# A fused attention and Fourier-mixing kernel: the row blocks of a second column half in another order, fewer stored pieces, sums of b beside other projections

## The chip, the cores and the metric

The kernel runs on one core of one Trainium2 chip. The metric is the device time of one execution in microseconds (us). The kernel before was executed three times; its median is 2955.21 us, from 2953.21 to 2961.31 us. A further execution was taken by the hardware profiler: it took 2959.83 us, with a span of 2958.1 us from its first to its last instruction, and every view of the profile shows that one.

## The reference

Two layers with inputs of their own stand side by side in the output.

```
qkv = x @ wqkv                          # x 2048 x 1024, wqkv 1024 x 3072, 32 heads of 32
p   = softmax(q @ k.T * 32 ** -0.5)
A   = concat_heads(p @ v) @ wo          # 2048 x 1024

a   = x @ dft_hid_re.T ;  b = x @ dft_hid_im.T     # another x, 2048 x 1024
B   = dft_seq_re @ a - dft_seq_im @ b              # 2048 x 1024
out = concatenate([A, B], -1)
```

All is float32. The DFT matrices are ordinary inputs: the kernel multiplies by them.

## The kernel before, in words

**Products in pieces of three.** A float32 operand is split into a high part and a low part of a shorter float type: `halves` (L491) makes the high part by a cast (VectorE or ScalarE, L497 and L499) and the low part by a subtraction (GpSimd or VectorE, L502). `group` (L401) then issues three matmuls for each pair of 128 x 128 by 128 x 512 tiles (high by high, low by high, high by low) into one PSUM bank, all of them at L412. The left operand of a group is a `piece` (L508): 128 x 512 floats, raw, high ("h") and low ("l"); the high and low tiles come from two rings of four buffers each (`HR`, `LR`, L419). The right operand is `moving` (L534) and lies in numbered slots (`slot`, `take_slot`).

**Fewer products.** The matrix products use a seven-product scheme for 2 x 2 blocks (the products are numbered 1 to 7 and taken in `ORDER` = 1, 2, 5, 6, 7, 3, 4). Products 5, 6, 7 and 3 need sums of blocks. A sum is made from loaded blocks by `fetch` (L439, addition at L477), and sums that are needed again are stored to DRAM and loaded back.

**The stages**, in the order of TensorE's work list `fills`:

1. `qkv` (L622): the projections to q, k and v in twelve steps. Steps 0 to 4 make what the first heads need; step 5 is product 1 for the other five column blocks, 6 is product 2, 7 is product 6, 8 is product 5, 9 is product 3; steps 10 and 11 (products 7 and 4) do v and then q and k, eight blocks with four groups each. From about 200 us on attention runs beside it.
2. `dense1` (L1486), the sequence DFT of B on the 2048 x 1024 input before the hidden one. It has 14 outer products `(r, pp)`: r = 0 (cosine matrix) with seven pp, then r = 1 (sine matrix) with seven. For r = 0 an outer product is done as a plain 4 x 2 block product (L1611 to L1658): two column halves n, in each four row blocks m, in each two pieces (k = 0, 1) with four chunks, so 24 matmuls a group and 192 an outer product. For r = 1 the seven-product scheme is applied a second time (L1659 to L1675), 14 groups of 12 matmuls.
3. `dense2` (the hidden DFT) and the attention's output projection `project`, `project_end`.

Attention's matmuls are three streams (scores "S" at L1786, transposed scores "T" at L1908, values "V" at L1927), interleaved with the list `fills`.

**Pieces stored and read again.** For r = 0, column half n = 0 makes its eight pieces (raw, cast, subtraction) and stores each, high and low part, to `ha_d` (`keep_a`, L1243); n = 1 reads all eight back (`again`, L1580, loads at L1594). The stored pieces with keys 1, 2 and 4 are read once more for r = 1; those with key 0 are not. Beside r = 0, `aside_c` (L1267) makes eight further pieces an outer product for r = 1 (products 5, 6, 3 and 7): it loads blocks into three small tiles "c" (L1289), adds (L1295), splits (L1296, L1297) and stores two halves to `ha_d` (L1298). One call of `aside_c` follows each group. `a_piece` (L1236) would make a piece for r = 1 that was not stored so far, and store it too.

**Sums of b beside the projections.** `aside` (L1306) makes sums of blocks of the sine matrix that r = 1 needs: two loads (L1333), one addition (L1335), one store to `tg_d` or `tb_d` (L1341), in a slot of its own out of three. `todo_a` lists 64 of them (16 for each of the outer products 5, 6, 7 and 4); 30 are done, one after each q and k group of steps 5, 6 and 7. The others are made by `load_r` (L1527) when r = 1 needs them; a sum that was made ahead is loaded there as one block.

**Who orders the work.** A planner (`Plan`, L62) simulates the five engines while the kernel is built, and what it starts in its time is the fixed program order of each engine. TensorE takes the heads of the streams or the next entry of `fills`. On the other engines, the operation with the smallest `rank` among those that are ready goes first; a rank is the number of groups built so far, plus an offset: `AHEAD` = 2 for `aside`, `LATER` = 6 for `aside_c`, negative for the attention's small loads. A DMA is planned to end at `dma + kb / KB_US + LANDING` (L145) with `KB_US` = 360 KB/us, and SP may issue only while the planned DMA time is less than `QUEUE` ahead (L217). On the chip each engine works through its order and waits on semaphores; every load and store but a few is issued by SP, in that order.

Of the kernel before, what the change touches and what calls it, by code (L numbers as in the profile page):

```python
# [61 lines left out]
class Plan:  # L62
# [6 lines left out]
    OVERLAP = {"ACT": 0.13, "DVE": 0.08, "POOL": 0.08}  # L69

    SLACK = {("SP", "POOL"): 2.0, ("SP", "DVE"): 2.0, ("SP", "PE"): 2.0, ("POOL", "DVE"): 0.7}
    KB_US = 360.0
    LANDING = 1.6
    QUEUE = 1.0

# [54 lines left out]
    def start(self, o, e=None):  # L130
# [11 lines left out]
        if o.kb:  # L142
            for _ in range(o.lanes):
                t = max(self.free[e], self.lane[0])
                self.dma = max(self.dma, t) + o.kb / o.lanes / self.KB_US  # L145
                o.end = self.dma + self.LANDING
# [74 lines left out]
def kernel(  # L221
# [46 lines left out]
    def f(ap):  # L268
        return ap.bitcast(F32)
# [82 lines left out]
    TWO = {(1,q) for q in ORDER}  # L352
# [74 lines left out]
    def seq():  # L427
        return float(len(frees))
# [153 lines left out]
    def chunk(p, c):  # L582
        return p, lambda t: t[:, c, :]
# [22 lines left out]
    def accs(i):  # L606
        old, users = take_slot(i)
        box = {}

        def get():  # L610
            if "t" not in box:
                box["t"] = slot(i, [P, 2, NB], F32)
            return box["t"]

        return [Acc(get, old, users, k) for k in range(2)]
# [6 lines left out]
    def qkv():  # L622
# [46 lines left out]
        def acc(i):  # L669
            box = {}  # L670

            def get():
                if "t" not in box:
                    box["t"] = vp.tile([P, 2, NB], F32, name=f"acc{i}")
                return box["t"]

            return [Acc(get, [], [], k) for k in range(2)]
# [161 lines left out]
        def qk_group(x, W, b, n, order=None):  # L839
            p = STEPS[x][0]  # L840
            early = x < 5
            h = FIRST.get(p)
            if p == 1 and n == 0:
                if early:
                    X[2 * b], X[2 * b + 1] = acc(b)
                else:
                    X[2 * b], X[2 * b + 1] = accs(15 + b - PAIRS)

            group(((chunk(W[c], b) if x == 0 else chunk(W, c), (XS[x, 4 * n + c], whole)) for c in range(4)), 4,
                  gather(p, 2 * b + n, qk_result(b + 8 * h[0], 2 * h[1] + n, early) if h else None, early, None if b % 2 else SCALE), order)  # L850
            if 5 <= x < 8:
                aside((12, 13, 14))
            elif x == 10 and b < 0:
                aside((0, 1, 2))

        def v_group(x, t):
# [379 lines left out]
    def a_piece(pp, p, i):  # L1236
        s = lambda x: (si_d[0][pp][x - 5][i], si.setdefault((pp, x, i), []))
        terms = a_terms(pp, p, i)
        a = piece(terms, s(p) if p in (5, 6) else None)
        keep_a(a, pp, p, i)  # L1240
        return a

    def keep_a(a, pp, p, i):  # L1243
        rank = seq()
        kept_a[pp, p, i] = [op("SP", ISSUE, lambda k=k, t=t: nc.sync.dma_start(ha_d[pp][p][i][:, k * NB : k * NB + NB], f(t()).rearrange("p t c -> p (t c)")), [made], [u], rank, 256)
                            for k, (t, made, u) in enumerate(zip((a.hi, a.lo), a.made, a.users.lists))]
# [15 lines left out]
    def put_b(r, pp, j):  # L1262
        return pp, "b", r, j
# [37 lines left out]
    kept_a = {}  # L1301

    todo_a = [put_b(1, pp, j) for pp in ORDER if pp in (5, 6, 7, 4) for j in range(16)]
    AHEAD, EACH, LATER = 2, 1, 6

    def aside(places):  # L1306

# [178 lines left out]
    def dense1():  # L1486
        spare[0] = True

        outers = [(r, pp) for r in range(2) for pp in ORDER]
        xo, yo = ([[[] for _ in range(8)] for _ in range(2)] for _ in range(2))  # L1490
        R, M, L, XY = [], {}, {}, {}
        PURE = [r for r in range(2) if not any((r, q) in TWO for q in ORDER)]
        NR = 12
# [105 lines left out]
        for o, (r, pp) in enumerate(outers):  # L1599
            hh = QUAD.get(pp)  # L1600

            def place_of(h, i):
                pos = 4 * h[0] + 2 * i + h[1] if h else 0
                to = wrote = None
                if h and hh:
                    c, nt = 2 * h[0] + i, 2 * hh[1] + h[1]
                    to = g_d[r][hh[0]][nt][:, :, c, :].rearrange("t p c -> p t c")
                    wrote = g_st[r][hh[0]][nt]
                return (xo_d[r][pos], xo[r][pos]), (yo_d[r][pos], yo[r][pos]), to, wrote

            if (r, pp) not in TWO:  # L1611
                for n in range(2):
                    for m in range(4):
                        r1, i = divmod(m, 2)

                        def terms():
                            for k in range(2):
                                key = {(0, 0): 1, (0, 1): 2, (1, 1): 4, (1, 0): 0}[r1, k]
                                if (pp, key, i) in kept_a:
                                    a = again(pp, key, i)  # L1620
                                else:
                                    a = piece([a_outer(pp, m, k)])
                                    keep_a(a, pp, key, i)
                                if m == k == 0 and L.get((o, n, 7)) is None:
                                    for c in range(NR - 8, 8):
                                        load_l(2 * o + n, c)
                                for c in range(4):
                                    yield chunk(a, c), (L[o, n, 4 * k + c], whole)

                        pos = 4 * r1 + 2 * i + n  # L1630
                        if r in PURE and pp in (1, 5) and n == 0 and i == 0 and r1 == 0:
                            XY[pp] = [None] * 8
                        if r in PURE and pp in (1, 5) and XY[pp][pos] is None:
                            XY[pp][pos & 6 : (pos & 6) + 2] = accs((16 if pp == 1 else 12) + pos // 2)
                        group(terms(), 8, gather1(pp, *place_of((r1, n), i), XY[1][pos] if r in PURE else None, XY[5][pos] if r in PURE and pp in (5, 7, 4) else None))
                        g = 2 * o + n
                        for c in range(NR - 8):
                            if c * 4 // (NR - 8) == m:
                                load_l(g + 1, c)
                                if g == 27:  # L1640
                                    load_ab(0, c)
                        if m == 3:
                            if n and o < 13 and outers[o + 1] in TWO:
                                while todo_c and todo_c[0][1] != 5:
                                    aside_c()
                                todo_c.clear()
                            if n and o < 13 and outers[o + 1] in TWO:
                                begin(o + 1, range(8))
                        if m == 1 and n and r in PURE and pp == 4 and o < 13 and outers[o + 1] in TWO:
                            load_r(o + 1, 0, 0)  # L1650
                            load_r(o + 1, 0, 1)
                            for kk in range(4):
                                load_b(o + 1, 0, kk)
                            early.append(1)
                        if r == 0 and (1, pp) in TWO:
                            todo_c.extend((pp, p, i) for p in {(0, 2): (5, 6, 3, 7), (0, 3): (5, 6, 3, 7)}.get((n, m), ()))
                        aside_c()
                continue  # L1658
            for x, p in enumerate(ORDER):  # L1659
                if p == 1:  # L1660
                    X = accs(10)
                if p == 5:
                    Y = accs(11)
                for i in range(2):
                    a = again(pp, p, i) if (pp, p, i) in kept_a else a_piece(pp, p, i)
                    group(((chunk(a, c), (M[o, x, c], whole)) for c in range(4)), 4, gather2(pp, p, X[i], Y[i] if p not in (1, 2) else None, *place_of(QUAD.get(p), i)))
                    if x < 6:
                        for kk in (2 * i, 2 * i + 1):
                            load_b(o, x + 1, kk)
                    elif o == 13:  # L1670
                        begin(14, range(4 * i, 4 * i + 4))
                    elif outers[o + 1] in TWO:
                        begin(o + 1, (2 * i, 2 * i + 1))
                    elif i:
                        begin(o + 1, range(8))  # L1675
# [294 lines left out]
    for h in range(H):  # L1970
        if h + 1 < H:
            scores(h + 1)
        else:
            sums(h)
        result(h, *transposed(h))
    dense1()
    dense2()
    project_end()
# [8 lines left out]
    while nf < len(fills) or any(place[n] < len(s) for n, s in streams.items()):  # L1987
# [43 lines left out]
        if nf < len(fills):  # L2031
            o, first, left = fills[nf]
# [14 lines left out]
        if ok:  # L2047
            n = min(ok)[1]
            o = heads[n][0]
# [49 lines left out]
```

## Time and profile before

| what | us |
|---|---|
| median of three executions | 2955.21 |
| profiled execution, its own time | 2959.83 |
| span of the profiled execution | 2958.1 |
| TensorE busy | 2924.5 |
| VectorE busy | 2378.0 |
| ScalarE busy | 2370.3 |
| GpSimd busy | 1124.1 |

The DMA engines moved 758.78 MB, 257 GB/s over the span. In a view of stretches of time, each row gives a stretch, then for each engine its busy time and in brackets its instructions, then the clock granted to TensorE, the mean busy share of the 16 DMA engines and their GB/s. A row of waits gives who waited for whom, the sum, the times and the longest. PE is TensorE, DVE VectorE, ACT ScalarE, POOL GpSimd, SP the engine that issues DMAs ("SPq" its queue). Matmuls overlap in the records, so a stretch can look busy while fewer matmuls start in it: the counts in brackets are the better measure.

### The profile page before, as it was taken

Reading aid. Unit: us, or ns where it says so; the run is one execution under the profiler, and the core shown is the slowest. Engines: PE = TensorE matmul, PEld = TensorE weight load, DVE = VectorE, ACT = ScalarE, POOL = GpSimd, SP = SyncE. Lnnn points to the kernel's source line nnn. Section 1 sums busy time; section 2 is a strip of 40 time slices with the busy share of each in tenths; the row PEclk is TensorE's granted clock in tenths of the full one; section 3 lists DMA queues with packets and bytes.
Section 4 is the critical chain, followed back from the end, with each engine's and each line's share of the span. In section 5 each row is a group of like instructions: output and inputs, shape, how many; then the busy total and the mean of one; then the engine's idle time right before and its main releaser. Section 6 shows DMA issues by size and latency. Waiting matters only on the chain.

```text
span 2958.1 us, 47210 instructions
## 1 busy us (share of the span) xinstructions
PE 2924.5 (99%) x14776; PEld 2120.4 (72%) x14776; DVE 2378.0 (80%) x3249; ACT 2370.3 (80%) x4487; POOL 1124.1 (38%) x883
## 2 busy tenths in 40 slices
PE   9999999999999999999999999999999999999999
PEld 8887677677776776666777776767777777777677
DVE  7678788778877888887799888888778887888655
ACT  5358798888888898888888898889888988888631
POOL 2325344132233444333356666667223512333000
PEclk9999999999999999999999999999999999999999
DMA  9979968667879999999988778886556555775468
GB/s 367 351 236 321 331 220 267 222 216 237 283 249 304 331 344 331 333 323 327 299 264 257 246 257 258 260 275 192 148 164 195 168 187 174 249 236 170 152 225 290
DMA packets 510614, 758.78 MB, mean 257 GB/s; under 512 B 123134, under 2 KB 156158, under 8 KB 510238
## 3 DMA queue, kind: packets, MB, share of 16 engines
q1 hardware_dynamic: 510220, 755.61, 77.9%
q8 instruction: 120, 1.97, 0.3%
q14 instruction: 130, 1.06, 0.1%
q10 hardware_dynamic: 144, 0.13, 0.0%
HBM read 509.64 MB, written 245.91 MB: 255 GB/s over the span
## 4 chain that ended last, share of the span: by engine, by line
PE 85%; DMA 9%; DVE 3%; ACT 1%; SPq 1%; issue 1%; POOL 1%; DVEq 0%; POOLq 0%; ACTq 0%
PE pd L412 39%; PE psT L1908 14%; PE psS L1786 13%; PE pd L1927 13%; PE psT L412 5%; DMA ha_d<-c 2%; DVE negm L1792 1%; DMA g<-in_ct 1%; DMA raw<-in_ct 1%; ACT psS L1795 1%; DMA slot<-tg_d 0%; DMA h<-ha_d 0%; DMA tg_d<-slot 0%; DMA l<-ha_d 0%; DMA qs<-m_d 0%
## 5 line engine op out<-in xcount | busy, mean ns | idle before, releaser
L1792 DVE TENSOR_REDUCE negm<-psS 128x1 f32<-128x1024 f32 x1024 | 1241.9, 1220 | 194.8 <-PE psS L1786 188.7
L1912 ACT ACTIVATE pt<-psT 128x512 f32<-128x512 f32 x2048 | 1186.7, 664 | 254.7 <-PE psT L1908 252.3
L1795 ACT ACTIVATE psS<-psS,negm 128x1024 f32<-128x1024 f32 x1024 | 1182.4, 1155 | 73.8 <-DVE negm L1792 70.6
L412 PE MATMUL pd<-slot,h 128*128 128x512 f32 x3392 | 1155.4, 391 | 3.7 <-DVE e L682 3.0
L1908 PE MATMUL psT<-qs,ks 128*128 128x512 f32 x2048 | 806.2, 397 | 8.1 <-DMA qs<-m_d 4.3
L412 PEld LDWEIGHTS pd<-slot,h 128*128 128x128 f32 x3392 | 639.5, 189 | 138.4 <-DVE e L682 3.3
L412 PE MATMUL pd<-slot,l 128*128 128x512 f32 x1696 | 662.8, 391 | 5.1 <-DMA l<-ha_d 2.7
L1908 PEld LDWEIGHTS psT<-qs,ks 128*128 128x128 f32 x2048 | 383.1, 188 | 170.0 <-issue 54.5
L1786 PE MATMUL psS<-ks,qs 128*128 128x512 f32 x1552 | 476.0, 393 | 7.5 <-ACT psS L1795 7.4
L1927 PE MATMUL pd<-pt,vt 128*32 128x512 f32 x4096 | 460.4, 596 | 0.6 <-DVE e L977 0.2
L412 PEld LDWEIGHTS pd<-slot,l 128*128 128x128 f32 x1696 | 319.5, 188 | 73.3 <-DMA l<-ha_d 3.5
L502 POOL TENSOR_TENSOR slot<-raw,slot 128x512 fp32r<-128x512 f32 x151 | 193.7, 1290 | 434.5 <-DVE slot L499 100.3
L1786 PEld LDWEIGHTS psS<-ks,qs 128*128 128x128 f32 x1552 | 289.8, 188 | 74.5 <-ACT psS L1795 16.4
L1927 PEld LDWEIGHTS pd<-pt,vt 128*32 128x32 f32 x4096 | 123.6, 110 | 284.6 <-issue 265.4
L477 POOL TENSOR_TENSOR raw<-raw,g 128x512 f32<-128x512 f32 x143 | 184.9, 1296 | 358.7 <-DVE negm L1792 49.8
L1795 ACT ACTIVATION_READ_ACCUMULATOR psS<-psS,negm 128x1 f32 x1024 | 279.7, 273 | 0.0
L502 POOL TENSOR_TENSOR l<-raw,h 128x512 fp32r<-128x512 f32 x110 | 141.9, 1290 | 293.0 <-PE psT L1908 69.2
L502 POOL TENSOR_TENSOR slot<-slot,slot 128x512 fp32r<-128x512 f32 x149 | 190.2, 1292 | 139.6 <-DVE slot L502 29.6
L412 PE MATMUL pd<-slot,slot 128*128 128x512 f32 x780 | 212.0, 390 | 0.2 <-DVE e L734 0.2
L412 PEld LDWEIGHTS pd<-slot,slot 128*128 128x128 f32 x780 | 146.5, 188 | 31.1 <-DVE e L734 0.9
L1786 PE MATMUL psS<-ks,qx 128*128 128x512 f32 x496 | 151.6, 396 | 3.2 <-ACT psS L1795 1.8
L477 DVE TENSOR_TENSOR raw<-raw,g 128x512 f32<-128x512 f32 x133 | 100.9, 763 | 27.0 <-issue 7.1
(139 smaller groups left out, 2278.2 us busy)
## 6 DMA issues: line engine op xcount, KB each, us to landing
h<-ha_d SPq DMA_DIRECT2D x154, 256.0 KB
l<-ha_d SPq DMA_DIRECT2D x154, 256.0 KB
slot<-in_ct SPq DMA_DIRECT2D x112, 256.0 KB
ha_d<-c SPq DMA_DIRECT2D x112, 256.0 KB
qk_d<-e SPq DMA_DIRECT2D x52, 512.0 KB
qs<-qk_d SPq DMA_DIRECT2D x128, 192.0 KB
ks<-qk_d SPq DMA_DIRECT2D x128, 192.0 KB
raw<-in_ct SPq DMA_DIRECT2D x96, 256.0 KB
```

The costliest lines, as they stand in the source:

```text
L412: nc.tensor.matmul(box["ps"], a[1]((a[0].hi, a[0].lo)[u]()), b[1]((b[0].hi, b[0].lo)[v]()), start=k == 0, stop=k == n - 1)
L477: (nc.gpsimd if e == "POOL" else nc.vector).tensor_tensor(out=dest(), in0=dest() if a is None else a.get(), in1=other["q"] if "q" in other ...
L502: (nc.gpsimd if e == "POOL" else nc.vector).tensor_tensor(out=lo(), in0=raw(), in1=f(hi()), op=ALU.subtract)
L1786: nc.tensor.matmul(p[:, i * NB : i * NB + NB], (QX[0] if own else QS[h % 2])[:, qt * P : qt * P + P], KS[h % 2][:, c * 1024 + i * NB : c * ...
L1792: nc.vector.tensor_reduce(out=ST["negm"][:, c, qt : qt + 1], in_=box["p"], axis=AX.X, op=ALU.max, negate=True)
L1795: nc.scalar.activation(box["p"], box["p"], AF.Exp, bias=ST["negm"][:, c, qt : qt + 1], accum_out=ST["sums"][:, c, qt : qt + 1])
L1908: nc.tensor.matmul(box["p"], KS[h % 2][:, t * P : t * P + P], QS[h % 2][:, j * NB : j * NB + NB], start=True, stop=True)
L1912: nc.scalar.activation(box["t"], box["p"], AF.Exp)
L1927: nc.tensor.matmul(po["p"][j * DH : j * DH + DH, :], VT[h][:, k, :], box["t"], start=(k == t0), stop=(k == t), tile_position=(0, j * DH),)
```

## The change

For r = 0 the second column half takes its row blocks in the order 2, 3, 0, 1. The pieces of blocks 2 and 3, made last in the first half, are used again from their ring buffers (`stay`); only those of blocks 0 and 1 are read back. Pieces with key 0 are no longer stored. What hung on the row block's number (loads of the next right operands, the flush at the end) hangs on the turn instead. `a_piece` no longer stores. The sums of b follow only the first of each block's two q and k groups, in steps 5 to 8 (20 of them), and then every q and k group of step 10 (16, in slots 0 to 2): 36 in all. Two planner constants change: `KB_US` from 360 to 335, `LATER` from 6 to 3.

```
-    KB_US = 360.0
+    KB_US = 335.0
...
-            if 5 <= x < 8:
+            if 5 <= x < 9 and n == 0:
                 aside((12, 13, 14))
-            elif x == 10 and b < 0:
+            elif x == 10:
                 aside((0, 1, 2))
...
         a = piece(terms, s(p) if p in (5, 6) else None)
-        keep_a(a, pp, p, i)
         return a
...
-    AHEAD, EACH, LATER = 2, 1, 6
+    AHEAD, EACH, LATER = 2, 1, 3
...
             if (r, pp) not in TWO:
+                stay = {}
                 for n in range(2):
-                    for m in range(4):
+                    for turn, m in enumerate((2, 3, 0, 1) if n else (0, 1, 2, 3)):
                         r1, i = divmod(m, 2)
...
                                 key = {(0, 0): 1, (0, 1): 2, (1, 1): 4, (1, 0): 0}[r1, k]
-                                if (pp, key, i) in kept_a:
+                                if (m, k) in stay:
+                                    a = stay[m, k]
+                                elif (pp, key, i) in kept_a:
                                     a = again(pp, key, i)
                                 else:
                                     a = piece([a_outer(pp, m, k)])
-                                    keep_a(a, pp, key, i)
-                                if m == k == 0 and L.get((o, n, 7)) is None:
+                                    if key:
+                                        keep_a(a, pp, key, i)
+                                    if r1:
+                                        stay[m, k] = a
+                                if turn == k == 0 and L.get((o, n, 7)) is None:
                                     for c in range(NR - 8, 8):
                                         load_l(2 * o + n, c)
...
                         for c in range(NR - 8):
-                            if c * 4 // (NR - 8) == m:
+                            if c * 4 // (NR - 8) == turn:
                                 load_l(g + 1, c)
...
-                        if m == 3:
+                        if turn == 3:
...
-                        if m == 1 and n and r in PURE and pp == 4 and o < 13 and outers[o + 1] in TWO:
+                        if turn == 1 and n and r in PURE and pp == 4 and o < 13 and outers[o + 1] in TWO:
```

## The prediction, on record before the result

> **What bounds the kernel now.** First the page: how busy TensorE is, and the DMA line over 40 slices.
>
> ```profile
> span 2958.1 us, 47210 instructions
> PE 2924.5 (99%) x14776; PEld 2120.4 (72%) x14776; DVE 2378.0 (80%) x3249; ACT 2370.3 (80%) x4487; POOL 1124.1 (38%) x883
> DMA  9979968667879999999988778886556555775468
> ```
>
> TensorE looks full, and the change takes no matmul away, so a gain can only come from matmuls that start late. Overlapping records hide those; I count them. The chain of work gives the price of one instruction in an undisturbed run, 5.44 / 24 = 0.2267 us, and 4.43 / 40 = 0.1107 us for the V products:
>
> ```profile
> 24.88 5.44 PE psT L412 x24
> 282.45 4.43 PE pd L1927 x40
> ```
>
> Then the view of stretches, once for all instructions and once for the V products (L1927) alone. The counts in the first bracket are what to read.
>
> ```profile
> core 0: us, PE busy (x) PEld busy (x) DVE busy (x) ACT busy (x) POOL busy (x), PEclk, DMA share, GB/s
> 200.00:400.00 200.00, 192.26 (x922) 140.33 (x921) 157.21 (x200) 159.92 (x300) 91.53 (x71) 0.98 0.89 295
> 580.00:780.00 200.00, 200.00 (x1029) 145.28 (x1026) 165.53 (x226) 174.21 (x335) 51.41 (x41) 1.00 0.72 236
> 900.00:1300.00 400.00, 390.56 (x1986) 273.41 (x1979) 331.37 (x436) 347.98 (x658) 160.29 (x125) 1.00 0.98 330
> 1300.00:1500.00 200.00, 195.09 (x991) 136.72 (x990) 161.84 (x224) 169.27 (x325) 73.97 (x58) 0.99 0.94 307
> 1500.00:1800.00 300.00, 300.00 (x1553) 216.58 (x1555) 265.48 (x373) 265.98 (x513) 189.39 (x150) 1.00 0.80 258
> 1800.00:2000.00 200.00, 195.50 (x1014) 136.40 (x1007) 171.82 (x233) 169.99 (x324) 131.74 (x104) 0.98 0.83 266
> ```
>
> ```profile
> 200.00:400.00 200.00, 23.35 (x208) 0.98 0.89 295
> 580.00:780.00 200.00, 33.60 (x300) 1.00 0.72 236
> 900.00:1300.00 400.00, 68.07 (x608) 1.00 0.98 330
> 1300.00:1500.00 200.00, 34.07 (x304) 0.99 0.94 307
> 1500.00:1800.00 300.00, 52.37 (x468) 1.00 0.80 258
> 1800.00:2000.00 200.00, 39.34 (x344) 0.98 0.83 266
> ```
>
> Work done from 1500 to 1800: (1553 - 468) x 0.2267 + 468 x 0.1107 = 297.8 us, so 2.2 us are lost, 0.75 in 100: the normal state. The same sum gives 20.3 lost from 900 to 1300 (17.3 above normal), 10.6 from 1300 to 1500 (9.1 above), 15.1 from 200 to 400 (13.6 above), 10.0 from 1800 to 2000 (8.5 above), 1.5 from 580 to 780 (none). Some 48 us above normal in all; that is all there is to win.
>
> From 900 to 1500 r = 0 of the sequence DFT runs. What TensorE waits for from 750 to 1500 is spread out:
>
> ```profile
> PE psS L1786 <- ACT psS L1795: 5.1, 7, 1.2
> PE psT L1908 <- DMA qs<-m_d: 4.3, 3, 2.2
> PE psT L1908 <- ACT pt L1912: 3.7, 4, 1.2
> PE pd L412 <- DMA l<-ha_d: 0.6, 1, 0.6
> ```
>
> None of these says "the piece was late". But ScalarE and VectorE work in order, and their casts and sums of loaded blocks stand ahead of the exponentials; SP, in order too, issues the 16 KB load qs<-m_d between 256 KB ones. I read all of it as DMA time, because the queue has none left:
>
> ```profile
> 1000.00:1225.00 225.00, 219.40 (x1127) 152.21 (x1129) 190.22 (x252) 198.96 (x377) 97.13 (x76) 1.00 1.00 348
> ```
>
> Share 1.00 at 348 GB/s: that is the ceiling of this mix of loads and stores.
>
> **Does traffic explain the loss?** Counting transfers of 256 KB (0.262 MB) in the code for one outer product of r = 0: right operands 16 (product 1, 2, 3), 32 (7, 4) or 48 (5, 6); pieces 8, or 24 where they are sums; 16 stores and 16 loads of pieces in ha_d; 28 of `aside_c`; 8 stores of results except in 1, 5, 6; 11 for attention (a head moves 2,496 KB by the code, and 468 V products at 128 a head are 1.17 heads in 96 us). Products 5 and 6 come to 143, 7 to 135, 3 and 4 to 119, 2 to 103, 1 to 95. TensorE's pace for `fills` is
>
> ```profile
> 1500.00:1800.00 300.00, 174.95 (x601) 1.00 0.80 258
> ```
>
> 2.0 a us, so 192 matmuls last 96 us. At 348 GB/s products 5 and 6 need 143 x 0.262 / 0.348 = 107.7 us each, 12 too many, and 7 needs 101.7, 6 too many: 30 us, where these three stand (about 965 to 1270) and 17.3 us are lost. The others fit (119: 89.6 us).
>
> **Pieces that stay.** Four of eight pieces an outer product are not read back, and the two with key 0 are not stored: 8 loads and 4 stores. That is 12 of 143, and 56 loads and 28 stores in all:
>
> ```profile
> h<-ha_d SPq DMA_DIRECT2D x154, 256.0 KB
> l<-ha_d SPq DMA_DIRECT2D x154, 256.0 KB
> ha_d<-c SPq DMA_DIRECT2D x112, 256.0 KB
> ha_d<-h SPq DMA_DIRECT2D x56, 256.0 KB
> ha_d<-l SPq DMA_DIRECT2D x56, 256.0 KB
> ```
>
> I expect 126, 126, 112, 42 and 42 after. 5 and 6 then need 131 x 0.262 / 0.348 = 98.7 us, 3 too many; 7 needs 92.7 and fits. 30 becomes 6. Scaled to the measured 17.3 that leaves 3.5: **-14 us**. From 1300 to 1500 (307 GB/s, share 0.94) traffic fits on average; the stalls are local, and taking a tenth away may leave all 9.1 or none; I take half, **-4.5 us**. No other engine loses work: a piece read back had no cast and no subtraction. The buffers are no tighter: the four `h` and `l` buffers hold the pieces of blocks 2 and 3 until the second turn of the second half ends; the pieces of blocks 0 and 1 replace them one by one, loaded a group ahead as before. At the change of halves there are now no piece loads beside the four right operands that wait for the slots of the last group. The groups' sums go into accumulators of their own, so the order doesn't matter to them.
>
> **a_piece without a store** is worth nothing: ha_d<-c x112 is 7 x 8 pieces x 2, so each piece of r = 1 is already kept, and a_piece isn't reached.
>
> **Sums of b.** Each is two loads, an addition (20 of the 30 on GpSimd) and a store; the first fence is the view of tg_d and of L1335, the second TensorE's waits from 185 to 450.
>
> ```profile
> L1341 SPq DMA_DIRECT2D tg_d<-slot x30: 319/376/1604, 222.5 to 369.1; - x30
> L1335 POOL TENSOR_TENSOR slot<-slot x20: 1277/1288/1470, 220.7 to 366.3; 128x512 f32<-128x512 f32 x20
> ```
>
> ```profile
> PE pd L412 <- DVE e L682: 3.0, 1, 3.0
> PE pd L412 <- POOL l L502: 2.5, 1, 2.5
> ```
>
> Fifteen leave steps 5 to 7 (five return in step 8, to about 420 us): 45 x 0.262 = 11.8 MB of the 59 MB from 200 to 400 (295 GB/s x 200 us), a fifth. The two waits are for an evacuation and a low part, not for a sum; I take a fifth of 13.6, **-2.7 us**, between none and all. Sixteen come to the q and k groups of step 10 (580 to 780): 48 transfers, 12.6 MB, lift 236 to 299 GB/s. The nearest rows at such a rate, 295 and 307 GB/s, lose 13.6 and 9.1 us above normal in 200 us; the row at 258 loses none. So the price lies between 0 and 13.6; I take **+4**, well below the nearest rows, since a pair of pieces there feeds 48 matmuls where steps 5 to 9 need a new one after every 24. GpSimd has room (51 of 200 us). On SP the sums go ahead of loads for later groups; behind them wait the first right operands of r = 0, whose slots 0 to 2 they hold. The three slots take five or six sums each and should be free before 780. If not, three loads and splits (some 7 us) come on top. r = 1 saves the additions of six sums, beside a TensorE that loses nothing at 1500 to 1800: 0.
>
> **The two constants.** 360 KB/us is 368.6 GB/s, above the measured 348; 335 is 343.0, just below. The order planned with 343 should put fewer early waits into the in-order engines; I count this in the -4.5. At the start the queue moves more,
>
> ```profile
> 25.00:100.00 75.00, 75.00 (x333) 62.13 (x332) 55.85 (x78) 30.67 (x51) 23.26 (x18) 1.00 1.03 379
> ```
>
> but TensorE's order is a fixed list there and it is never idle: 0. A new plan also moves every chance stall, 1800 to 2000 among them: bounds +-8.5 (that stretch's excess), value 0. `LATER` 3 is the rival below.
>
> **Sum:** -14 - 4.5 - 2.7 + 4 = -17.2 from 2959.83, 2942.6. The profiled execution stands 4.6 above the median, so the forecast is 2955.2 - 17.2 = **2938 us**, its own range 2925 to 2947.
>
> **The clock.** Two of the three waits for qs<-m_d (the chain has these loads) stand just ahead of two stretches with a lower clock:
>
> ```profile
> 1226.53 4.38 DMA qs<-m_d
> 1398.73 3.33 DMA qs<-m_d
> ```
>
> ```profile
> 1225.00:1250.00 25.00, 23.23 (x115) 16.69 (x108) 19.80 (x30) 19.23 (x36) 5.58 (x5) 0.93 0.97 295
> 1400.00:1425.00 25.00, 22.89 (x96) 18.55 (x100) 16.34 (x18) 20.59 (x41) 7.57 (x6) 0.93 0.93 303
> ```
>
> 0.93 over 25 us is 1.75 us lost after a gap of about 2 us, so such a gap costs nearly double, and the losses above hold both halves. The Trainium skill, TensorE: Matmul & The Clock Gate, section "HAM oscillation — how this bites in real kernels", asks for "no PE-idle gaps >~3.4µs"; by it these two gaps (at most 2.2 us) would cost no clock, and the forecast without the 3.5 us would be 2941. The trace disagrees with that bound.
>
> **Rivals.** *Traffic isn't the limit of r = 0*: the waits at TensorE name ScalarE and a 16 KB load, and 10.6 us are lost from 1300 to 1500 where the queue isn't full. Then products 5 to 7 recover a third of the 14 us, 1300 to 1500 nothing, the new sums cost 4: -5 + 4 - 1 = -2, **2953**. Against it: the loss begins where the share reaches 1.00. The Trainium skill, DMA: Bandwidth & Descriptors, section "Bandwidth", measures 425 GB/s on a single core for large loads, and names some 358 GB/s as the HBM limit of a core; by 425, products 5 and 6 would need 88 us, nothing would be late, and this rival would hold. The trace, 348 at share 1.00, speaks for the second figure. Chance 0.18.
>
> *Slower: SP stuck on aside_c.* From 900 to 1500:
>
> ```profile
> SPq L1289 <- DMA ha_d<-c: 53.9, 32, 4.1
> ```
>
> SP stops until a store has landed before it may load the tile "c" again, 32 times of 48, and all that is behind it in its order waits: heads, right operands, qs<-m_d. With `LATER` 3 these loads stand three groups earlier in SP's order, nearer to their store. If every one of 48 waited 2.3 us instead of 1.1 (the longest is 4.1), the sum is 110 us. If the 26.4 us above normal all came from the 53.9 us (0.49 each), that is +27 on top of the sum, -17.2 + 27 = +9.8: **2965**. It decides from about 107 us of this wait (53.9 + (17.2 + 8.9) / 0.49). Against it: 343 GB/s also plans the landing later. Chance 0.15.
>
> *All stalls fall*: with the new rate also 1800 to 2000 (8.5) and most of 200 to 400, and no cost of the sums: -35, **2920**. Chance 0.14. The forecast keeps 0.53. That the change doesn't do what it says is excluded for the stores and loads, which the code counts, and true of a_piece.
>
> **Chances.** This kernel's executions differ by 0.3%, 8.9 us; less can't be told from no change. Faster: 0.51 of the forecast, 0.14, 0.02 of the first rival: 0.67. Same: 0.02 + 0.16 = 0.18. Slower: 0.15. Range 2918 to 2962: from the full recovery to short of the slow rival.
>
> **What would show it.** Right: 126, 126, 42, 42 transfers; 36 sums; from 900 to 1300 less than 8 us lost by the count and a DMA share under 0.95; 580 to 780 near 0.9 with under 7 us lost. Wrong: share still 1.00 from 1000 to 1225; the SP wait at L1289 above 90 us; clock rows under 1.00 at new places; a stall at the first groups of r = 0 near 780.

## The result, and the profile after

The changed kernel took 2926.59 us (median of 4 executions, 2922.56 to 2927.65) against 2955.90 (4 executions): ratio 0.9896, 95% interval 0.9879 to 0.9913, 29 us faster. The forecast was 2938, with a range from 2918 to 2962. The page of the profiled execution (2926.61 us):

```profile
span 2924.8 us, 47119 instructions
PE 2910.0 (99%) x14776; PEld 2116.9 (72%) x14776; DVE 2364.0 (81%) x3226; ACT 2363.7 (81%) x4489; POOL 1152.8 (39%) x904
DMA  9979958798768999999887677885456555775468
```

The span is 33.3 us shorter than that of the profiled execution before, which lay some 4 us above its median; TensorE's instructions are as many as before. So the count of instructions in each stretch has to show where the time went. The view of stretches, all instructions, then the V products alone (line 1932 of the changed kernel):

```profile
200.00:400.00 200.00, 199.83 (x976) 149.22 (x975) 167.50 (x217) 170.49 (x322) 82.46 (x64) 1.00 0.77 258
580.00:780.00 200.00, 199.87 (x1045) 142.29 (x1044) 167.28 (x229) 172.31 (x331) 75.68 (x59) 1.00 0.90 306
900.00:1300.00 400.00, 398.48 (x2063) 284.41 (x2062) 345.63 (x463) 358.52 (x684) 172.10 (x135) 1.00 0.93 311
1300.00:1500.00 200.00, 199.09 (x1035) 138.67 (x1035) 167.37 (x222) 177.04 (x340) 85.54 (x67) 1.00 0.87 284
1500.00:1800.00 300.00, 299.43 (x1551) 215.47 (x1550) 264.03 (x372) 263.86 (x508) 180.18 (x142) 1.00 0.77 247
1800.00:2000.00 200.00, 195.51 (x995) 138.24 (x994) 170.37 (x221) 173.98 (x333) 140.01 (x110) 0.99 0.77 245
```

```profile
200.00:400.00 200.00, 23.35 (x208) 1.00 0.77 258
580.00:780.00 200.00, 37.71 (x336) 1.00 0.90 306
900.00:1300.00 400.00, 71.77 (x640) 1.00 0.93 311
1300.00:1500.00 200.00, 37.71 (x336) 1.00 0.87 284
1500.00:1800.00 300.00, 52.92 (x472) 1.00 0.77 247
1800.00:2000.00 200.00, 34.91 (x296) 0.99 0.77 245
```

With the prediction's prices (0.2267 us, and 0.1107 for a V product) and its normal loss of 0.75 in 100, the loss above normal is now 1.4 us from 200 to 400 (13.6 before), 0.6 from 580 to 780 (0), 3.6 from 900 to 1300 (17.3), 2.8 from 1300 to 1500 (9.1), 7.3 from 1800 to 2000 (8.5). The first and the two of r = 0 make up -32.2 of the -33.3 us.

The waits of TensorE from 750 to 1500 had summed to some 14 us and now sum to some 2 us; from 1000 to 1225 the share of the DMA engines fell from 1.00 to 0.95 (second fence; the third is SP's wait from 900 to 1500):

```profile
PE psS L1791 <- ACT psS L1800: 0.8, 1, 0.8
PE psT L1913 <- ACT pt L1917: 0.7, 1, 0.7
PE pd L412 <- DVE l L502: 0.4, 1, 0.4
PE psT L1913 <- DMA qs<-m_d: 0.3, 1, 0.3
```

```profile
1000.00:1225.00 225.00, 223.48 (x1149) 160.00 (x1148) 196.54 (x267) 204.00 (x391) 102.65 (x80) 1.00 0.95 322
```

```profile
SPq L1288 <- DMA ha_d<-c: 55.5, 32, 3.0
```

The transfers are those forecast, 126 and 126 loads, 42 stores each of high and low parts, 36 sums:

```profile
h<-ha_d SPq DMA_DIRECT2D x126, 256.0 KB
l<-ha_d SPq DMA_DIRECT2D x126, 256.0 KB
```

```profile
L1244 SPq DMA_DIRECT2D ha_d<-h x42: 319/382/937, 738.1 to 1385.7; - x42
L1244 SPq DMA_DIRECT2D ha_d<-l x42: 319/382/1299, 738.6 to 1386.2; - x42
```

```profile
L1340 SPq DMA_DIRECT2D tg_d<-slot x32: 319/402/793, 222.6 to 651.1; - x32
```

```profile
L1340 SPq DMA_DIRECT2D tb_d<-slot x4: 320/352/386, 651.9 to 684.5; - x4
```

But from 200 to 400, 12.2 us were won where 2.7 were forecast. Theory at this point: less traffic in r = 0 and sums that no longer crowd steps 5 to 7. Rival: the planner's rate, 343 GB/s for 369, which the prediction had priced at nothing of its own.

### The profile page after: what moved, and what is told of

The parts are those of the page before. It is cut to its first block, busy times and chain, and to the rows that moved or that the text cites. A ratio compares the mean times of both kernels' runs of the same rounds, so it can differ in the third digit from the quotient of the medians.

```text
span 2924.8 us, 47119 instructions
## 1 busy us (share of the span) xinstructions
PE 2910.0 (99%) x14776; PEld 2116.9 (72%) x14776; DVE 2364.0 (81%) x3226; ACT 2363.7 (81%) x4489; POOL 1152.8 (39%) x904
## 4 chain that ended last, share of the span: by engine, by line
PE 94%; DMA 2%; DVE 1%; ACT 1%; issue 0%; POOL 0%; SPq 0%; DVEq 0%; ACTq 0%; POOLq 0%
PE pd L412 43%; PE psT L1913 15%; PE psS L1791 15%; PE pd L1932 15%; PE psT L412 5%; ACT psS L1800 1%; DMA raw<-in_ct 1%; DMA g<-in_ct 1%; DVE negm L1797 1%; DMA yo_d<-c 0%; ACT pt L1917 0%; POOL slot L502 0%; DMA slot<-tg_d 0%; DMA g<-in_xb 0%; DMA o_d<-ot 0%
## 5 line engine op out<-in xcount | busy, mean ns | idle before, releaser
L1800 ACT ACTIVATE psS<-psS,negm 128x1024 f32<-128x1024 f32 x1024 | 1195.1, 1167 | 70.4 <-DVE negm L1797 68.6
L412 PE MATMUL pd<-slot,h 128*128 128x512 f32 x3392 | 1150.8, 390 | 0.6 <-DMA h<-ha_d 0.6
L412 PEld LDWEIGHTS pd<-slot,h 128*128 128x128 f32 x3392 | 636.8, 188 | 134.9 <-DVE negm L1797 1.0
L412 PE MATMUL pd<-slot,l 128*128 128x512 f32 x1696 | 660.3, 390 | 0.9 <-POOL l L502 0.5
L412 PEld LDWEIGHTS pd<-slot,l 128*128 128x128 f32 x1696 | 318.4, 188 | 68.2 <-POOL l L502 1.1
L502 POOL TENSOR_TENSOR slot<-raw,slot 128x512 fp32r<-128x512 f32 x161 | 206.2, 1291 | 371.7 <-DVE slot L499 159.3
L1791 PEld LDWEIGHTS psS<-ks,qs 128*128 128x128 f32 x1552 | 289.9, 188 | 70.2 <-ACT psS L1800 11.8
L477 POOL TENSOR_TENSOR raw<-raw,g 128x512 f32<-128x512 f32 x154 | 200.1, 1304 | 300.4 <-ACT slot L497 31.9
L1800 ACT ACTIVATION_READ_ACCUMULATOR psS<-psS,negm 128x1 f32 x1024 | 292.2, 285 | 0.0
L412 PE MATMUL pd<-slot,slot 128*128 128x512 f32 x780 | 211.1, 389 | 0.0
L412 PEld LDWEIGHTS pd<-slot,slot 128*128 128x128 f32 x780 | 146.3, 188 | 30.7 <-DVE e L734 0.3
L1945 DVE TENSOR_TENSOR ot<-ot,pd 128x512 f32<-128x512 f32 x64 | 43.9, 687 | 88.6 <-PE pd L1932 88.3
```

Source lines behind the costliest of these rows:

```text
L412: nc.tensor.matmul(box["ps"], a[1]((a[0].hi, a[0].lo)[u]()), b[1]((b[0].hi, b[0].lo)[v]()), start=k == 0, stop=k == n - 1)
L477: (nc.gpsimd if e == "POOL" else nc.vector).tensor_tensor(out=dest(), in0=dest() if a is None else a.get(), in1=other["q"] if "q" in other ...
L502: (nc.gpsimd if e == "POOL" else nc.vector).tensor_tensor(out=lo(), in0=raw(), in1=f(hi()), op=ALU.subtract)
L1791: nc.tensor.matmul(p[:, i * NB : i * NB + NB], (QX[0] if own else QS[h % 2])[:, qt * P : qt * P + P], KS[h % 2][:, c * 1024 + i * NB : c * ...
L1800: nc.scalar.activation(box["p"], box["p"], AF.Exp, bias=ST["negm"][:, c, qt : qt + 1], accum_out=ST["sums"][:, c, qt : qt + 1])
L1945: nc.vector.tensor_tensor(out=po["o"], in0=po["o"], in1=po["p"], op=ALU.add)
```

## The experiments

The ratios are to the kernel before, timed beside each of them; the row "after" is the result above. Two ratios must differ by some 0.0023 to be told apart. The table gives the loss above normal of each profiled execution by the same count, in us. "Old" sums are the 30 of the kernel before; "stay" and "read back" say what happens to the pieces.

| kernel | rate, LATER, sums, pieces | ratio (95%) | 200-400 | 580-780 | 900-1500 | 1500-1800 | 1800-2900 |
|---|---|---|---|---|---|---|---|
| before | 360, 6, old, read back | 1 | 13.6 | 0.0 | 26.4 | 0.0 | 9.7 |
| s_stay | 360, 6, old, stay | 0.9998 (0.9987-1.0009) | 10.7 | -0.4 | 13.1 | 12.7 | 11.2 |
| s_asides | 360, 6, moved, read back | 1.0031 (1.0018-1.0044) | 7.7 | 5.2 | 37.9 | 2.5 | 5.2 |
| s_rate | 335, 6, old, read back | 0.9936 (0.9921-0.9951) | 7.7 | 0.1 | 10.9 | 6.8 | 3.6 |
| s_later | 360, 3, old, read back | 1.0007 (0.9993-1.0020) | 15.0 | -0.4 | 24.8 | 0.0 | 7.5 |
| u_rate | 360, 3, moved, stay | 0.9961 (0.9946-0.9976) | 6.1 | 6.1 | 12.6 | 0.9 | 12.1 |
| k345 | 345, 3, moved, stay | 0.9924 (0.9909-0.9939) | 5.0 | 6.6 | 9.7 | 0.2 | 8.6 |
| after | 335, 3, moved, stay | 0.9896 (0.9879-0.9913) | 1.4 | 0.6 | 6.4 | 0.9 | 7.9 |
| k310 | 310, 3, moved, stay | 0.9916 (0.9901-0.9931) | 0.7 | -0.2 | 12.9 | 2.6 | 1.2 |
| u_stay | 335, 3, moved, read back | 0.9930 (0.9913-0.9947) | 1.1 | 0.3 | 27.0 | 1.1 | 3.2 |
| u_asides | 335, 3, old, stay | 0.9943 (0.9927-0.9960) | 6.8 | -0.1 | 17.4 | 0.1 | 7.6 |
| u_later | 335, 6, moved, stay | 0.9930 (0.9914-0.9947) | 1.4 | 0.3 | 6.3 | 11.8 | 8.7 |
| g335_l360 | 335 for SP's pace, 360 for landing, 3, moved, stay | 0.9967 (0.9953-0.9980) | 5.0 | 1.4 | 15.9 | -0.2 | 12.8 |
| land26 | 360, landing 1 us later, 3, moved, stay | 0.9997 (0.9987-1.0007) | 4.8 | 2.5 | 5.8 | 23.8 | 10.5 |

How far can one execution's count be trusted? Up to 765 us the traces of before, s_stay and s_later show the same instructions in the same order on every engine, and so do those of after, u_stay and u_later. From 200 to 400 the first three lose 13.6, 10.7 and 15.0, the others 1.4, 1.1 and 1.4. So at the rate 360 a difference of 4 us between two rows of that column says little; how far r = 0 varies in one order was not measured.

**Each part alone.** s_stay has the row-block order, `stay` and no stores of key 0, as the change's diff has them, with the other parts left as they were.

> The order 2, 3, 0, 1 with pieces that stay and no stores of key 0, alone on the kernel before. Traffic theory: 126 loads of h and of l and 42 + 42 stores, the share from 1000 to 1225 falls under 0.97, the loss above normal from 900 to 1500 goes from 26.4 to about 10 us, 200 to 400 keeps its 13.6: about -16, ratio 0.9946. Rival (the planned rate did it): the orders still count on 369 GB/s, more than half of the 26.4 us stays: -8 at most, ratio 0.997.

Its stretches in r = 0 and just behind it, all instructions and then the V products (line 1932):

```profile
900.00:1300.00 400.00, 395.85 (x2033) 282.77 (x2035) 336.69 (x450) 350.49 (x669) 181.86 (x142) 1.00 0.92 306
1300.00:1500.00 200.00, 196.22 (x1017) 137.80 (x1010) 161.30 (x219) 168.12 (x322) 83.05 (x66) 1.00 0.85 270
1500.00:1800.00 300.00, 293.92 (x1499) 207.08 (x1499) 264.17 (x373) 255.94 (x491) 169.90 (x134) 0.98 0.79 251
```

```profile
900.00:1300.00 400.00, 69.00 (x616) 1.00 0.92 306
1300.00:1500.00 200.00, 35.99 (x324) 1.00 0.85 270
1500.00:1800.00 300.00, 53.84 (x472) 0.98 0.79 251
```

r = 0 did gain about what the traffic account says, 26.4 to 13.1 (about 10 was expected), but the whole kernel gained nothing, 0.9998 where 0.9946 or 0.997 was expected: 12.7 us were given back in one place just behind. TensorE's order of time there:

```profile
1620.00 0.61 PE L1791 MATMUL psS<-ks,qx 128*128 128x512 f32 x2
1621.95 0.73 PE L1791 MATMUL psS<-ks,qx 128*128 128x512 f32 x2 [1.34 <-ACT psS L1800]
1624.08 1.22 PE L1791 MATMUL psS<-ks,qx 128*128 128x512 f32 x2 [1.40 <-ACT psS L1800]
1625.10 1.06 PE L1913 MATMUL psT<-qs,ks 128*128 128x512 f32 x2
1625.97 1.22 PE L1791 MATMUL psS<-ks,qx 128*128 128x512 f32 x2
1626.99 0.63 PE L1913 MATMUL psT<-qs,ks 128*128 128x512 f32 x1
1628.31 1.22 PE L1791 MATMUL psS<-ks,qx 128*128 128x512 f32 x2 [0.70 <-ACT psS L1800]
```

There is no L412 in it. From 1620.0 to 1642.2 us the program order holds attention alone, 15 us of scores and transposed scores and then 48 V products: the planner put no entry of `fills` there. The kernel has two PSUM tiles for scores, so a score can't be made before the exponentials of the last but one are done, and TensorE waits 0.7 to 1.4 us at nearly every one. The waits name no load: this is a hole in the order. Why the planner had nothing to put there was not looked into. The same waits, just behind 1600, are in u_later (11.8) and land26 (23.8), and not in the others. TensorE's waits from 1500 to 1800, u_later first, then land26:

```profile
PE psS L1791 <- ACT psS L1800: 5.6, 6, 1.4
```

```profile
PE psS L1791 <- ACT psS L1800: 10.0, 15, 1.1
```

s_asides has only the two `aside` conditions of the change.

> Only the sums of b moved (20 in steps 5 to 8, 16 in step 10), on the kernel before. If the sums caused the stalls from 200 to 400: that stretch's loss above normal goes from 13.6 to about 2, 580 to 780 from 0 to under 2, about -11, ratio 0.996. If the planned rate did it: 200 to 400 keeps about 10 us and 580 to 780 gains 2 to 4, ratio 0.999 to 1.001. 900 to 1500 keeps its 26 us in both.

Two stretches, all and V products (line 1927):

```profile
200.00:400.00 200.00, 194.78 (x948) 142.99 (x947) 162.70 (x204) 165.24 (x310) 87.69 (x67) 1.00 0.77 257
580.00:780.00 200.00, 196.03 (x1004) 140.16 (x1003) 163.92 (x220) 174.07 (x335) 64.04 (x50) 1.00 0.85 293
```

```profile
200.00:400.00 200.00, 23.35 (x208) 1.00 0.77 257
580.00:780.00 200.00, 33.21 (x296) 1.00 0.85 293
```

Half of each theory: 200 to 400 gains 5.9 (the share falls from 0.89 to 0.77), and 580 to 780 pays 5.2 (share 0.85, 0.72 before). r = 0 is worse by 11.5 with the same bytes, which neither theory expected; the part alone makes the kernel slower, 1.0031 where 0.996 or 0.999 to 1.001 was expected.

s_rate and s_later change one constant each:

```
-    KB_US = 360.0
+    KB_US = 335.0
```

> Only KB_US from 360 to 335, on the kernel before. Traffic theory: the same bytes; 900 to 1500 recovers at most a quarter of 26.4 (-6), 200 to 400 at most 3: ratio 0.997 to 1.000. Rival (the planned rate did it): 900 to 1500 loses under 14 and 200 to 400 under 4: about -20, ratio 0.993.

The ratio is the rival's, 0.9936. So is r = 0, 10.9 where the rival had under 14; but 200 to 400 keeps 7.7, where it had under 4. In r = 0, all and V products (line 1927):

```profile
900.00:1300.00 400.00, 395.22 (x2031) 277.35 (x2029) 339.29 (x464) 352.89 (x677) 155.62 (x121) 1.00 0.97 327
1300.00:1500.00 200.00, 200.00 (x1047) 142.60 (x1046) 164.76 (x213) 177.15 (x341) 89.95 (x72) 1.00 0.96 320
```

```profile
900.00:1300.00 400.00, 71.78 (x640) 1.00 0.97 327
1300.00:1500.00 200.00, 37.71 (x336) 1.00 0.96 320
```

The queue is as full as before (0.97, 327 GB/s; before 0.98, 330), and 10.8 us are lost there for 17.3, and 0.1 for 9.1 behind. So the loss wasn't just a full queue: with the same bytes, another order loses 15.5 us less (6.8 of them are lost again from 1500 to 1800). My theory, that the constant has no worth of its own, fell here.

```
-    AHEAD, EACH, LATER = 2, 1, 6
+    AHEAD, EACH, LATER = 2, 1, 3
```

> Only LATER from 6 to 3, on the kernel before. Both theories: within 3 us, ratio 0.999 to 1.001. My slow rival: the SP wait for ha_d<-c from 900 to 1500 rises from 53.9 to over 90 us, and the time by over 9 us, ratio 1.003 or more.

Ratio 1.0007, and SP's wait from 900 to 1500 fell a little (from 53.9), so the slow rival has neither its wait nor its time:

```profile
SPq L1289 <- DMA ha_d<-c: 46.4, 31, 2.7
```

**One part undone in the changed kernel.** u_rate, k345 and k310 set `KB_US` in it to 360, 345 and 310.

> The changed kernel with KB_US back at 360: order, stay, sums moved and LATER 3 remain. Theory now (the planned rate decides how much of the saved traffic reaches TensorE): stalls return wherever the queue is busy; of the 29 us at least 18 are lost, ratio to the kernel before 0.996 to 1.002, loss above normal over 200 to 2000 at 30 us or more. Rival (the parts add up, the rate is worth 0.6% alone): 0.9896 + 0.0064 = 0.996.

> The changed kernel with KB_US 345 (353 GB/s planned, against 348 measured at a full queue before). If the rate's worth is a smooth match to the ceiling: between 0.990 and 0.993. If 335 is a lucky order: anywhere from 0.989 to 1.000, with the loss in single events.

> The changed kernel with KB_US 310 (317 GB/s planned). If landing late in the plan only costs lead: 0.989 to 0.991, as 335. If too low a rate holds loads back: over 0.993. If 335 is a lucky order: anywhere up to 1.000.

0.9961, 0.9924, 0.9896 and 0.9916 for 360, 345, 335 and 310: the rate is worth 0.65% in the changed kernel, 0.64% alone. u_rate meets both expectations (33.5 us above normal from 200 to 2000, and 0.996), so it doesn't tell them apart; and 0.9936 alone times 0.9961 for the rest is 0.9897. But only the totals add up, not the stretches: alone the rate wins 15.5 us in r = 0 and has nothing to win from 580 to 780; in the changed kernel it wins 6.2 and 5.5. The column 580 to 780 is the clearest: with the sums there it costs 5.2 to 6.6 us at 360 and 345, and 0.6 or less at 335 and 310. With the moved sums, 200 to 400 falls with the rate, 6.1, 5.0, 1.4, 0.7. k345 lies in the range of a smooth match, k310 between its cases. 310 is not clearly worse than 335 (0.0020 between them). Its losses stand elsewhere: before 200 us, where TensorE's list is fixed, its count gives 11.2 us above normal against 2.6 in the changed kernel, and r = 0 loses 12.9.

u_stay goes back to the old order of row blocks with all pieces stored and read back.

> The changed kernel without the pieces part: old order of row blocks, all pieces stored and all read back; KB_US 335, LATER 3 and the moved sums remain. Theory: 154 and 154 loads, share near 1.00 from 1000 to 1225, loss above normal from 900 to 1500 at 10 to 16 us (6.4 with the part): ratio 0.992 to 0.994. Rival (stay is worth nothing, as alone): 0.9896 within 0.001.

0.9930, as the theory expected: the pieces part is worth 10 us at this rate, 3 to 17 with the noise of both ratios. r = 0 goes from 6.4 to 27.0, more than expected, and the share from 1000 to 1225 from 0.95 to 0.97. The larger part, 21.5 for 3.6, is lost from 900 to 1300 (all, then V products, line 1927):

```profile
900.00:1300.00 400.00, 390.48 (x1984) 271.78 (x1983) 334.89 (x447) 352.61 (x673) 150.08 (x117) 0.99 0.96 319
```

```profile
900.00:1300.00 400.00, 71.77 (x640) 0.99 0.96 319
```

u_asides and u_later put back the old places of the sums, and `LATER` 6.

> The changed kernel with the sums of b where they were (30, after every q and k group of steps 5 to 7). If moving them is worth what the stretch 200 to 400 shows beside rate alone: 200 to 400 back from 1.4 to about 7.7 us above normal, ratio 0.991 to 0.9925. If they are worth nothing at 335: 0.9896 within 0.001.

> The changed kernel with LATER back at 6. If LATER 3 helps the sequence DFT at the new pace: 900 to 1500 above 10 us (6.4 with 3), ratio 0.991 to 0.993. If it is nothing: 0.9885 to 0.9905. If 3 costs waits of SP, as my slow rival had it: under 0.9885.

u_asides: 200 to 400 at 6.8, as expected; but r = 0 lost 11 us more as well, so the ratio, 0.9943, is worse than expected. For 200 to 400 the runs now make a full square, since up to 765 us the order is the same in all runs of one rate and one place of the sums (means of these runs):

| 200 to 400, us above normal | rate 360 | rate 335 |
|---|---|---|
| old sums | 13.1 (before, s_stay, s_later) | 7.2 (s_rate, u_asides) |
| moved sums | 6.9 (s_asides, u_rate) | 1.3 (after, u_stay, u_later) |

Moving the sums is worth 6 at either rate, and the rate 6 with either place of the sums. u_later: ratio as the first case, reason not. Its r = 0 loses 6.3 (6.4 with 3); the 11 us are the hole near 1600. `LATER` 3 did nothing to the stage that it is meant for.

**What in the rate does it.** g335_l360 splits the constant: SP's pace is planned with 335, the landing with 360. land26 keeps 360 and plans each landing 1 us later.

```
-    KB_US = 335.0
+    KB_US, KB_LAND = 335.0, 360.0
...
-                o.end = self.dma + self.LANDING
-                self.lane = self.lane[1:] + [o.end]
+                self.dma2 = max(self.dma2, t) + o.kb / o.lanes / self.KB_LAND
+                o.end = self.dma2 + self.LANDING
+                self.lane = self.lane[1:] + [self.dma + self.LANDING]
```

```
-    KB_US = 335.0
-    LANDING = 1.6
+    KB_US = 360.0
+    LANDING = 2.6
```

> The changed kernel where the planner uses 335 KB/us only to hold SP back (when the next DMA may be issued) and 360 for the moment a load lands. Theory P (pace: the plan has to issue and consume at the pace the queue can keep): as 335, ratio 0.989 to 0.991, 580 to 780 under 2 us above normal. Theory D (the planned landing alone matters): as 360, ratio 0.994 to 0.997, 580 to 780 at 5 us or more.

> The changed kernel with KB_US 360 and a planned landing 1 us later (LANDING 2.6 in place of 1.6): same pace as 360, more lead. Theory P: 0.994 to 0.997, 580 to 780 at 5 us or more above normal. Theory D: 0.989 to 0.991, 580 to 780 under 2.

Neither theory holds as written: the split has the ratio of D (0.9967) and the 580 to 780 of P (1.4), land26 has neither (0.9997 and 2.5). Over 200 to 400, 580 to 780 and 900 to 1500, u_rate loses 24.8 us, the pace alone 22.3, the later landing 13.1, the rate for both (after) 8.4. In these three the later landing carries more, but the hole near 1600 takes more than that gain, so no ratio shows it. What in the rate does it is open.

## Why the prediction was right, and where its terms were not

**Size of r = 0: right.** -14 from 900 to 1300 and -4.5 behind were forecast, -13.7 and -6.3 came. The pieces alone did -9.7 and -3.6 (s_stay); undone in the changed kernel they cost 17.9 and 2.7 (u_stay). That the sum of -18.5 fits the measured -20.0 so well is in part luck: the rate alone did -15.5 in the same place, and what pieces and rate win there is not the sum of both.

**Its reason: half right.** The account of bytes put the whole loss on a queue that is late. s_rate loses 15.5 us less from 900 to 1500 with the same bytes. Over all runs, r = 0 loses 10.9 to 37.9 us with pieces read back (five kernels, mean 25.4) and 5.8 to 17.4 with pieces that stay (nine, mean 11.1). The part is worth about 14 us in the mean, 13.3 and 20.6 in the two pairs that differ in it alone, and an order can be worth as much again. It need not be: u_stay has the rate 335 too, and loses 27.0, 16 more than s_rate. The two differ in `LATER` and in the sums, and the runs point at the sums: where pieces are read back, moved sums go with 11.5 us more in r = 0 (s_asides beside before) and 16.1 (u_stay beside s_rate); where pieces stay, with 0.5 and 11.0 less (u_rate beside s_stay, after beside u_asides). `LATER` moves r = 0 by 1.6 us at most (s_later, u_later). Why it is so wasn't found.

**"The two constants"** is the step that failed. The prediction saw that 360 KB/us (369 GB/s) stands above the measured 348 GB/s, and still counted the remedy inside -4.5. Alone it is worth 0.64%, 19 us, and 0.65% in the changed kernel.

**Sums leaving steps 5 to 7, -2.7:** mis-sized. Moving them is worth about 6, the rate another 6 (the square above). A share of the bytes was the wrong measure.

**Sums beside step 10, +4:** near for 360 (5.2 and 6.1), near nothing at 335 (0.6). The prediction took the price from rows with a like rate, 295 and 307 GB/s, which lost 13.6 and 9.1 us; now 580 to 780 moves 306 GB/s and loses 0.6, and s_rate moves 320 from 1300 to 1500 and loses 0.1. The rate of a stretch alone doesn't set its loss.

**Other stretches, 0 within 8.5:** held for the change (0.9 and -1.8), but not for its neighbours: the hole near 1600 costs 12.7, 11.8 and 23.8 in three of them. The changed kernel escaped it, and 11 us of its lead over u_later and 12 of that over s_stay are this. Nothing in the prediction foresaw it, so that part is luck.

**Rivals.** "Traffic isn't the limit" had products 5 to 7 recover a third of 14 us; s_stay recovers 9.7 there, so it falls as it was written, but s_rate shows that it was right to doubt that traffic is all. "SP stuck on aside_c" falls with s_later and with 55.5 us after. "All stalls fall" (2920, chance 0.14) came nearer than the forecast: 2926.59 is 7 us above it and 11 below 2938. Most of 200 to 400 fell and the new sums cost next to nothing, as it says; its 1800 to 2000 did not fall (7.3 for 8.5). "a_piece without a store" changed no count: ha_d<-c is 112 on both sides, and the 14 stores fewer of h and of l are those of key 0.

**The sum** fell 12 us short of the medians, 16 of the profiled executions, because the errors pointed the same way: 9.5 us from 200 to 400, 3.4 from 580 to 780, 1.8 from 1300 to 1500. The rate is in all three.

## What to carry to other kernels

When a program fixes each engine's order from a model, the model's DMA rate is part of the kernel: compare it with the rate that the trace shows at a full queue, and try values below it. Here the trace showed 348 GB/s (and 379 from 25 to 100 us, with loads and stores too, so a full queue has no one rate); beside 343 planned, 353 and 369 were worse by 0.3% and 0.65%, and 317 can't be told from 343. Four values of one kernel don't show that the match itself is the cause. Look for the gain of a part by stretches and not by the whole time alone: s_stay saved 13 us in its stage and lost 13 in a hole that the new order opened elsewhere. And a part that costs by itself can be worth having beside others: the moved sums alone make the kernel slower (s_asides, 1.0031), and taking them out of the changed kernel does too (u_asides, 0.9943 for 0.9896).

## What the runs showed of the hardware

TensorE's granted clock fell to half after waits of under 1.5 us, and stayed there while TensorE was busy some 70 in 100 of the time. Stretches of 5 us in s_stay, in the hole shown above; the last three numbers are clock, DMA share and GB/s:

```profile
1615.00:1620.00 5.00, 5.00 (x24) 4.09 (x22) 4.88 (x12) 5.00 (x12) 3.13 (x3) 1.00 0.83 290
1620.00:1625.00 5.00, 2.26 (x7) 1.31 (x7) 4.90 (x10) 4.32 (x9) 2.64 (x3) 0.86 0.88 282
1625.00:1630.00 5.00, 3.84 (x8) 1.67 (x7) 5.00 (x6) 3.56 (x6) 2.98 (x4) 0.50 0.88 274
1630.00:1635.00 5.00, 3.29 (x6) 1.51 (x6) 5.00 (x6) 2.83 (x7) 3.74 (x4) 0.50 0.81 213
1640.00:1645.00 5.00, 5.00 (x31) 3.07 (x24) 1.85 (x2) 1.48 (x3) 1.29 (x1) 1.00 0.86 264
```

Behind two waits of 1.34 and 1.40 us the clock is 0.50, and a pair of score matmuls takes 1.22 us in place of 0.61. With a wait of some 0.7 us at most of them, the clock stays at 0.50 for 10 us; it comes back between 1635 and 1640 us (0.77 in that stretch), where dense V products run. In land26 it stays at 0.50 for 20 us:

```profile
1620.00:1630.00 10.00, 6.84 (x12) 3.16 (x12) 7.12 (x10) 6.57 (x13) 6.14 (x6) 0.50 0.51 154
1630.00:1640.00 10.00, 6.89 (x12) 3.19 (x13) 6.59 (x6) 6.46 (x11) 2.87 (x3) 0.50 0.74 229
```

The Trainium skill (TensorE: Matmul & The Clock Gate, section "Part 1: The HAM clock gate") has the clock halve after an idle window of some 3.4 us and come back after one busy window. The return agrees with these rows: the clock is back within 5 us of the start of the dense products. The fall does not need an unbroken 3.4 us of idleness here, since none of the waits shown is longer than 1.4 us.
